# A fourth buffer for the experts' second-layer weights, each load issued four steps ahead instead of three

## The chip, the cores and the metric

The kernel runs on one core of a Trainium2 chip. The metric is the device time of one execution in microseconds (us), lower is better. Before the change it is 457.55 us, the median of three runs (457.02 to 459.05). A core has TensorE (matmuls), VectorE, ScalarE and GpSimd for the rest of the arithmetic, and SyncE, whose queue issues the large transfers between the chip's memory (HBM) and the core's on-chip memory (SBUF). In the profile they are PE, DVE, ACT, POOL and SP; PEld is TensorE's loading of weights.

## What is computed

Three layers, one after the other, all in float32. The first is a retention attention: scores with a decay per head in place of a softmax, over 2 x 8 heads, 576 positions, head size 64. Its output, 1152 tokens of width 512, goes through a layer of 8 experts: a gate picks one expert for each token, and the token passes through that expert's two matrices. The result goes through a normalised, gated feed-forward of width 1536. Cut to the part that the change touches:

```python
logits = x @ w_gate                                  # 1152 x 512 by 512 x 8
expert_idx = np.argmax(logits, axis=1)
...
h = np.maximum(np.einsum('ecd,edf->ecf', disp, w1), 0.0)   # w1: 8 x 512 x 1024
y = np.einsum('ecf,efd->ecd', h, w2)                       # w2: 8 x 1024 x 512
...
out[i] = gate_w[i] * y[expert_idx[i], pos[i]]
```

## The kernel before, in words

The attention comes first (0 to 64 us in the trace). It writes each token's row into a table in HBM that is ordered by expert, so that the rows of one expert lie together. Then the experts run one after the other (about 65 to 219 us), those with the most tokens first, and last the feed-forward.

The experts' weights don't fit in SBUF at once, so they are streamed. An expert's work is cut into four **steps** of 256 hidden columns each, 32 steps in all (`steps`, line 994). A first-layer tile (`w1t`, 1 MB) serves two steps and lives in a ring of three buffers. A second-layer tile (`w2t`, 128 partitions x 2 x 512 float32, 512 KB) serves one step and lives in a ring of three buffers, `w2p` (line 141). The function `load_w2` (line 194) issues the load on SyncE's queue, and `next_w2` (line 983) takes the next tile from the list `w2_q`. The loads of the first three tiles are issued during the attention (`AT_LOADS`, line 34).

A second-layer tile is not used as it comes. So that TensorE can run in a faster format with float32's accuracy, the tile is split in two parts. `w2_hi` (line 753, two instructions at line 759 on ScalarE) makes the rounded part `w2h`, and `w2_lo` (line 762, one instruction at line 768 on VectorE) makes the rest, `w2l`. After both, the tile's buffer is free. Some steps split their first-layer weights as well (lines 782 and 788), and in the others TensorE reads `w1t` as it is (line 848).

The whole program is written out by hand in the order in which each engine is to take it (`manual_schedule`), and the program's loop over the steps (line 1000) sets that order. In step i:

- every second step issues a first-layer load (line 1002);
- `l1` multiplies the first layer of step i on TensorE (lines 841, 843 and 848). It writes the accumulator `hp`, of which there is one, so it waits until the step before has read it;
- `l1_sum`, `h_hi` and `h_lo` add the parts, apply the relu and split the result `h` (lines 857, 858, 871, 877);
- `w2_lo` of step i runs on VectorE, and right behind it `next_w2` issues the next second-layer load;
- `w2_hi` of step i+1 runs on ScalarE;
- `w1_hi` and `w1_lo` of step i+2 run, where that step splits its first layer;
- `l2` of step i-1 multiplies the second layer on TensorE (lines 896 and 897) into accumulators of which there is one set, so an expert's first step waits until `norm_a` has read out the expert before (`y`, line 923);
- between these stand the norms of the expert before, the rows of the expert after next (`load_x`, line 791, read by the transposes at line 809), and, in one step of four, a piece of converting the feed-forward's weights (`bg_ops`).

```python
        if not split(e, j):
            w2_lo(e, j)
        next_w2()
        ...
        for n in nxt:
            for _ in w2_hi(*n):
                pass
```

SyncE takes its queue in order. A second-layer load waits there for the `w2l` that frees its buffer; behind it stand the first-layer loads, the rows and the units of the feed-forward's weights (`st`, line 210). GpSimd issues a few transfers of its own: ten scatters of token numbers (line 988), one in each of steps 4 to 13.

Of the kernel before, what the change touches and what calls it, by code (L numbers as in the profile page):

```python
# [25 lines left out]
TW = 192  # L26
# [63 lines left out]
def kernel(  # L90
# [47 lines left out]
    xnp = ctx.enter_context(tc.tile_pool(name="xnp", bufs=1, side="right"))  # L138
    es_w = ExitStack()
    w1p = es_w.enter_context(tc.tile_pool(name="w1p", bufs=3, side="right"))  # L140
    w2p = es_w.enter_context(tc.tile_pool(name="w2p", bufs=3, side="right"))

    x0p = es_w.enter_context(tc.tile_pool(name="x0p", bufs=1, side="right"))

# [35 lines left out]
    xh = xnp.tile([P, KD, XW], F32R, name="xh")  # L180
    xl = xnp.tile([P, KD, XW], F32R, name="xl")

# [1 line left out]
    w1_t, w2_t, w2_s, w2u = {}, {}, {}, {}  # L184
    st_t = {}

# [7 lines left out]
    def load_w2(e, j):  # L194
        t = w2p.tile([P, 2, DM], F32, tag="w2", name="w2t")
        nc.sync.dma_start(out=t, in_=w2[ds(ex[e], 1), j * 256:(j + 1) * 256, :].rearrange("o (k p) f -> p (o k) f", p=P))
        w2_t[e, j] = t
# [92 lines left out]
            bg_ops(1)  # L290
        conv_tail()

# [1 line left out]
    dec = ap1.tile([P, NP * S], F32, name="dec")  # L294
    ubd = ap1.tile([P, NP, P], F32, name="ubd")
    wid = ap1.tile([P, KD, P + E], F32, name="wid")
# [269 lines left out]
    cnt, kept, inc, off, dn, dinc, zz, key, skey, over, few, perm, skept, offe = (fl[:, i, :] for i in range(14))  # L566
# [70 lines left out]
    def positions(n):  # L637
        for _ in range(min(n, len(pos_q))):
            pos_q.pop(0)()

# [1 line left out]
    def clear_rows(pool, r, r0):  # L642
        at = pool.tile([CW, 1], F32, tag="at", name="vat")
        xr = pool.tile([CW, XC], F32, tag="xr", name="vxr")
        ok = pool.tile([CW, 1], F32, tag="ok", name="vok")
        ri = pool.tile([CW, 1], I32, tag="ri", name="vri")
        tr = cst("trash", CW)[:, 0:1]
        nc.vector.memset(xr, 0.0)
        nc.vector.tensor_scalar(out=ok, in0=tr, scalar1=float(r0 - E * R), scalar2=skept[:CW, r:r + 1], op0=ALU.add, op1=ALU.is_ge)
        nc.vector.tensor_scalar(out=at, in0=perm[:CW, r:r + 1], scalar1=float(R), scalar2=float(r0 - E * R), op0=ALU.mult, op1=ALU.add)  # L650
        nc.vector.scalar_tensor_tensor(out=ri, in0=ok, scalar=at, in1=tr, op0=ALU.mult, op1=ALU.add)
        nc.gpsimd.indirect_dma_start(
            out=tab[:], out_offset=bass.IndirectOffsetOnAxis(ap=ri[:, 0:1], axis=0),
            in_=xr[:], in_offset=None)
# [75 lines left out]
        ints[0:1, 0:E], engines=[ENG.DVE], min_val=0, max_val=NT,  # L730
        skip_runtime_bounds_check_because="prefix sums of expert counts never exceed the number of tokens")

# [1 line left out]
    wA = ctx.enter_context(tc.tile_pool(name="wA", bufs=A_U))  # L734
    stg = ctx.enter_context(tc.tile_pool(name="stg", bufs=ST))
    cvt = ctx.enter_context(tc.tile_pool(name="cvt", bufs=3))
# [54 lines left out]
    def load_x(e):  # L791
        xr = mp1.tile([CW, 2, XC], F32, tag="xr", name="xr")
        w = WIDTHS[e]
        nc.sync.dma_start(out=xr[:w // 2], in_=tab[ds(ex[e] * R, w)].rearrange("(b p) c -> p b c", p=w // 2))
        xr_t[e] = xr
# [187 lines left out]
    def next_w2():  # L983
        if w2_q:
            load_w2(*w2_q.pop(0))
# [9 lines left out]
    for _ in w2_hi(*steps[0]):  # L995
        pass
    load_x(1)
    nps = {}
    positions(8)
    for i, (e, j) in enumerate(steps):  # L1000
# [63 lines left out]
    l2(*steps[-1])  # L1064
    es_w.close()

# [1 line left out]
    GT = 384  # L1068
    phases = [list(range(0, A_U)), list(range(A_U, A_U + PH1)), list(range(A_U + PH1, NF2))]
    order = [(ph, g, f) for ph in range(3) for g in range(NG) for f in phases[ph]]  # L1070
# [154 lines left out]
```

## Time and profile before

| | |
|---|---|
| median of three runs | 457.55 us |
| lowest, highest | 457.02, 459.05 us |
| profiled execution, first to last instruction (its span) | 453.2 us |
| the profiled execution's own time | not recorded beside its span |
| TensorE busy | 432.1 us (95%) |
| VectorE busy | 286.6 us (63%) |
| ScalarE busy | 210.8 us (47%) |
| GpSimd busy | 53.3 us (12%) |
| mean rate of the transfers | 160 GB/s |

Times in the trace count from the first instruction. A matmul's end is modelled, so neighbouring matmuls seem to overlap, and the distance from start to start tells more than the duration. The clock granted to TensorE in the experts' stage is 0.99 of full speed, which is the upper of its two levels, 2.4 GHz. An idle time in the trace stands with what ended it: `[0.96 <-DVE hb L858]` is 0.96 us without work, ended by VectorE's `hb`, line 858.

### The profile page before, as it was taken

The page shows a single profiled execution, that of the slowest core. Times are in us where ns is not written, and L with a number is a line of the kernel's source. Part 1 is how long each engine was busy: PE and PEld are TensorE (multiplying, and loading weights), DVE is VectorE, ACT ScalarE, POOL GpSimd, SP SyncE. Part 2 cuts the span into 40 slices and gives each one's busy share as a digit, 9 for nine tenths or more (in the row PEclk, how much of TensorE's full clock was granted, in tenths as well). Part 3 has the DMA queues.
Part 4 walks back from the last instruction along what each step waited for, and adds up shares of the span by engine and source line. Part 5 has one row for each costly group of instructions (what it writes and reads, how often), then busy time and mean ns, then how long its engine had stood idle before and what let it go on. Part 6 is the DMA issues. An engine that isn't in the chain of part 4 may idle for free.

```text
span 453.2 us, 7828 instructions
## 1 busy us (share of the span) xinstructions
PE 432.1 (95%) x2968; PEld 409.9 (90%) x2968; DVE 286.6 (63%) x677; ACT 210.8 (47%) x453; POOL 53.3 (12%) x45
## 2 busy tenths in 40 slices
PE   5999959999999998999999999999999999999994
PEld 5888859999998988999999999999999999999993
DVE  3899848678787877876588888793873113113212
ACT  3443326677686848766456665361441111111210
POOL 8005210122411011012000000000000002001102
PEclk9999989999999999999999999999999999999998
DMA  8999837897989796666025555251300001000101
GB/s 282 299 282 374 306 112 245 269 294 197 326 171 310 251 303 231 235 229 238 2 90 174 166 165 196 93 171 61 94 0 1 0 2 69 1 1 6 65 0 69
DMA packets 40448, 72.31 MB, mean 160 GB/s; under 512 B 3894, under 2 KB 16566, under 8 KB 40404
## 3 DMA queue, kind: packets, MB, share of 16 engines
q1 hardware_dynamic: 38580, 67.00, 46.5%
q0 software_dynamic: 1824, 4.75, 2.9%
q8 instruction: 25, 0.41, 0.4%
q14 instruction: 19, 0.16, 0.1%
HBM read 65.21 MB, written 6.52 MB: 158 GB/s over the span
## 4 chain that ended last, share of the span: by engine, by line
PE 66%; ACT 8%; DMA 7%; DVE 3%; issue 1%; POOL 1%; POOLq 0%; DVEq 0%; ACTq 0%
PE gv L1098 11%; PE gv L1099 11%; PE gv L1100 11%; PE hp L848 7%; DMA w2t<-in_moe_w_dram 7%; PE o L1132 5%; PE o L1134 5%; PE o L1133 5%; PE acc L896 5%; ACT w2h L759 2%; PE acc L897 2%; PE hp L841 1%; ACT xn L935 1%; ACT w1h L782 1%; ACT xt L817 1%
## 5 line engine op out<-in xcount | busy, mean ns | idle before, releaser
L1098 PE MATMUL gv<-xh,uh 128*128 128x384 f32 x280 | 94.9, 339 | 0.0
L1100 PE MATMUL gv<-xh,ul 128*128 128x384 f32 x280 | 94.7, 338 | 0.0
L1099 PE MATMUL gv<-xl,uh 128*128 128x384 f32 x280 | 94.7, 338 | 0.0
L896 PE MATMUL acc<-h,w2h 128*128 128x384 f32 (+6 forms) x256 | 72.0, 356 | 1.5 <-DVE y L923 1.4
L897 PE MATMUL acc<-h,w2l 128*128 128x192 f32 (+6 forms) x256 | 61.5, 240 | 0.0
L1110 DVE TENSOR_TENSOR sg<-sg,gv 128x384 f32<-128x384 f32 x35 | 19.3, 551 | 63.8 <-PE gv L1100 59.6
L848 PE MATMUL hp<-xt,w1t 128*128 128x192 f32 (+6 forms) x336 | 53.0, 313 | 4.9 <-PEq L713 2.9
L848 PEld LDWEIGHTS hp<-xt,w1t 128*128 128x128 f32 x336 | 49.2, 195 | 5.7 <-DVE ints L604 3.1
L1098 PEld LDWEIGHTS gv<-xh,uh 128*128 128x128 f32 x280 | 52.7, 188 | 1.4
L1099 PEld LDWEIGHTS gv<-xl,uh 128*128 128x128 f32 x280 | 52.7, 188 | 1.4
L1112 ACT ACTIVATE sh<-sg 128x384 fp32r<-128x384 f32 x36 | 18.9, 526 | 73.1 <-DVE sg L1110 73.0
L1100 PEld LDWEIGHTS gv<-xh,ul 128*128 128x128 f32 x280 | 52.7, 188 | 0.0
L896 PEld LDWEIGHTS acc<-h,w2h 128*128 128x128 f32 x256 | 48.1, 188 | 2.1 <-DVE y L923 2.1
L897 PEld LDWEIGHTS acc<-h,w2l 128*128 128x128 f32 x256 | 49.0, 191 | 0.0
L759 ACT ACTIVATE w2h<-w2t 128x512 fp32r<-128x512 f32 x64 | 36.6, 621 | 14.1 <-DMA w2t<-in_moe_w_dram 9.5
L1132 PE MATMUL o<-uh,sh 128*128 128x512 f32 x108 | 42.8, 397 | 0.0
L1134 PE MATMUL o<-uh,sl 128*128 128x512 f32 x108 | 42.7, 396 | 0.0
L1133 PE MATMUL o<-ul,sh 128*128 128x512 f32 x108 | 42.5, 394 | 0.0
L1108 ACT ACTIVATE sg<-gv 128x384 f32<-128x384 f32 x35 | 17.0, 486 | 49.5 <-PE gv L1100 49.5
L768 DVE TENSOR_TENSOR w2l<-w2t,w2h 128x1024 fp32r<-128x1024 f32 x32 | 38.9, 1215 | 0.0
L1147 POOL DMA_INDIRECT out_dram<-part,ids_sb x9 | 8.8, 982 | 215.1 <-DVE part L1145 214.2
L259 ACT ACTIVATE uh<-mag 128x512 fp32r<-128x512 f32 x36 | 22.6, 627 | 14.7 <-DVE mag L251 10.0
(172 smaller groups left out, 723.0 us busy)
## 6 DMA issues: line engine op xcount, KB each, us to landing
w1t<-in_moe_w_dram SPq DMA_DIRECT2D x16, 1024.0 KB, 9.5
w2t<-in_moe_w_dram SPq DMA_DIRECT2D x32, 512.0 KB, 7.1
st<-in_moe_w_gate_dram SPq DMA_DIRECT2D x12, 512.0 KB, 4.6
st<-in_moe_w_val_dram SPq DMA_DIRECT2D x12, 512.0 KB, 4.1
st<-in_moe_w_out_dram SPq DMA_DIRECT2D x12, 512.0 KB, 4.1
qkt<-in_qk_dram SPq DMA_DIRECT2D x6, 512.0 KB, 6.0
kvt<-in_kv_dram SPq DMA_DIRECT2D x6, 512.0 KB, 6.1
tab<-xh SPq DMA_DIRECT2D x9, 193.5 KB, 6.1
```

What stands on the lines that cost most here:

```text
L259: nc.scalar.activation(out=uh[:, s, :], in_=mag, func=ACTF.Copy)
L759: nc.scalar.activation(out=w2_s[e, j][0][:, a, :], in_=t[:, a, :], func=ACTF.Copy)
L768: nc.vector.tensor_tensor(out=lo, in0=t, in1=hi.bitcast(F32), op=ALU.subtract)
L848: nc.tensor.matmul(hp[:, a, 0:w], wt[:, kk, f * FT:(f + 1) * FT], xt[:, kk, :], start=(kk == 0), stop=(kk == KD - 1))
L896: nc.tensor.matmul(ac[d // 2][:, d % 2, 0:2 * w], hi[:, a, d * P:(d + 1) * P], h[:, a].rearrange("p s t -> p (s t)"), start=first, stop=Fa ...
L897: nc.tensor.matmul(ac[d // 2][:, d % 2, 0:w], lo[:, a, d * P:(d + 1) * P], h[:, a, 0, :], start=False, stop=last, skip_group_check=True)
L1098: nc.tensor.matmul(ps[:, 0:GT], w_h, x_h, start=(kk == 0), stop=False)
L1099: nc.tensor.matmul(ps[:, 0:GT], w_h, x_l, start=False, stop=False)
L1100: nc.tensor.matmul(ps[:, 0:GT], w_l, x_h, start=False, stop=(kk == KD - 1))
L1132: nc.tensor.matmul(o, a, uh[:, 2, :], start=(f == fs[0]), stop=False)
L1133: nc.tensor.matmul(o, a, ul[:, 2, :], start=False, stop=False)
L1134: nc.tensor.matmul(o, b, uh[:, 2, :], start=False, stop=(f == fs[-1]))
```

## The change

The ring of second-layer tiles gets a fourth buffer, and one call of `next_w2` is added ahead of the loop, so that each later call takes the tile after the one it took before. In step i the call issues tile i+4 instead of tile i+3. The buffer that it goes into is that of tile i, as before. The other lines of the diff only take out comments.

```diff
-    w2p = es_w.enter_context(tc.tile_pool(name="w2p", bufs=3, side="right"))
+    w2p = es_w.enter_context(tc.tile_pool(name="w2p", bufs=4, side="right"))
...
     for _ in w2_hi(*steps[0]):
         pass
     load_x(1)
+    next_w2()
     nps = {}
     positions(8)
     for i, (e, j) in enumerate(steps):
```

## Rows read from the trace of the kernel before

**Rows 1.** Busy time by stage: length, us of PE, PEld, DVE, ACT, POOL, clock, DMA.

```profile
65.00:219.00 154.00, 150.51 (x1131) 149.23 (x1130) 116.86 (x207) 107.78 (x234) 23.86 (x18) 0.99 0.79 245
...
177.00:205.00 28.00, 28.00 (x234) 28.00 (x232) 22.54 (x41) 20.96 (x47) 3.06 (x2) 1.00 0.71 244
```

**Rows 2.** Waits from 64 to 219 us: engine, line, what it waited for, us in total, times, longest.

```profile
ACT w2h L759 <- DMA w2t<-in_moe_w_dram: 9.5, 4, 3.1
```

**Rows 3.** ScalarE in order of time: start, duration, instruction, and in brackets the idle time before.

```profile
119.30 1.15 ACT L759 ACTIVATE w2h<-w2t 128x512 fp32r<-128x512 f32 x2 [2.26 <-DMA w2t<-in_moe_w_dram]
...
139.71 1.15 ACT L759 ACTIVATE w2h<-w2t 128x512 fp32r<-128x512 f32 x2 [3.10 <-DMA w2t<-in_moe_w_dram]
...
165.65 1.15 ACT L759 ACTIVATE w2h<-w2t 128x512 fp32r<-128x512 f32 x2 [2.59 <-DMA w2t<-in_moe_w_dram]
...
169.96 1.15 ACT L759 ACTIVATE w2h<-w2t 128x512 fp32r<-128x512 f32 x2 [1.57 <-DMA w2t<-in_moe_w_dram]
```

**Rows 4.** TensorE in order of time around its three idle times.

```profile
142.85 0.35 PE L896 MATMUL acc<-h,w2h 128*128 128x340 f32 x1
143.04 0.24 PE L897 MATMUL acc<-h,w2l 128*128 128x170 f32 x1
144.24 0.54 PE L848 MATMUL hp<-xt,w1t 128*128 128x162 f32 x2 [0.96 <-DVE hb L858]
...
167.67 0.24 PE L897 MATMUL acc<-h,w2l 128*128 128x162 f32 x1
168.95 0.40 PE L848 MATMUL hp<-xt,w1t 128*128 128x154 f32 x1 [1.04 <-DVE h L877]
...
170.63 0.69 PE L848 MATMUL hp<-xt,w1t 128*128 128x154 f32 x4
172.71 0.41 PE L896 MATMUL acc<-h,w2h 128*128 128x308 f32 x1 [1.40 <-DVE y L923]
```

**Rows 5.** Waits of SyncE's queue, whole span, same columns as rows 2.

```profile
SPq L196 <- DVE w2l L768: 98.4, 27, 5.2
```

**Rows 6.** SyncE's issues of second-layer loads, then us to landing (first two alike).

```profile
104.39 0.38 SPq L196 DMA_DIRECT2D w2t<-in_moe_w_dram  x1
...
125.08 0.37 SPq L196 DMA_DIRECT2D w2t<-in_moe_w_dram  x1
...
150.44 0.37 SPq L196 DMA_DIRECT2D w2t<-in_moe_w_dram  x1
...
154.52 0.37 SPq L196 DMA_DIRECT2D w2t<-in_moe_w_dram  x1
...
w2t<-in_moe_w_dram SPq DMA_DIRECT2D x1, 512.0 KB, 8.7
...
w2t<-in_moe_w_dram SPq DMA_DIRECT2D x1, 512.0 KB, 3.3
...
w2t<-in_moe_w_dram SPq DMA_DIRECT2D x1, 512.0 KB, 11.1
```

**Rows 7.** The first-layer load in step 0: issue, us to landing, first reader on ScalarE.

```profile
66.30 0.41 SPq L191 DMA_DIRECT2D w1t<-in_moe_w_dram  x1
...
w1t<-in_moe_w_dram SPq DMA_DIRECT2D x1, 1024.0 KB, 6.0
...
84.19 1.13 ACT L782 ACTIVATE w1h<-w1t 128x512 fp32r<-128x512 f32 x2
```

**Rows 8.** Two stretches, then a first-layer load's issue, us to landing, first read.

```profile
105.00:110.00 5.00, 5.00 (x40) 4.99 (x39) 4.79 (x6) 5.00 (x12) 0.01 (x1) 1.00 0.43 31
110.00:126.00 16.00, 16.00 (x116) 15.84 (x115) 12.49 (x23) 10.80 (x24) 6.79 (x4) 1.00 0.98 309
...
105.02 0.37 SPq L191 DMA_DIRECT2D w1t<-in_moe_w_dram  x1
...
w1t<-in_moe_w_dram SPq DMA_DIRECT2D x1, 1024.0 KB, 12.1
...
123.88 0.41 PE L848 MATMUL hp<-xt,w1t 128*128 128x170 f32 x1
```

## The prediction

> **What bounds the kernel now.** I read the busy time by stage first, because the change touches one stage only: the experts, 65 to 219 us. There TensorE is busy 150.51 of 154 us, so 3.49 us is all that it idles, while VectorE and ScalarE have over 37 us of slack each [rows 1]. From 177 to 205 us (the last step of expert 5, expert 6 and the first steps of expert 7) it has no gap at all: 28.00 of 28.00 us. The stage is thus bound by TensorE wherever the loads come in time, and whatever the change brings must come out of TensorE's gaps.
>
> Next I read the waits of the engines in this stage. ScalarE stood 9.5 us, in four waits, for a second-layer weight tile that had not landed [rows 2]. The reader should not take 9.5 us as the gain: ScalarE is not the bound. Its four waits are 2.26, 3.10, 2.59 and 1.57 us long [rows 3], before tiles 11, 15, 20 and 21 (I number the 32 tiles as the 32 steps, four to an expert).
>
> Then TensorE's own order of time around them [rows 4]. After the wait of 3.10 it idles 0.96 us for the sum `hb`, after the 2.59 it idles 1.04 us for `h`, after the 1.57 it idles 1.40 us for `y`. All three are made on VectorE from something that stands behind the late `w2h` split in ScalarE's order of instructions. These three make 3.40 of the 3.49 us. The wait of 2.26 shows no idle time behind it. So ScalarE can be roughly 1.4 to 2 us late before TensorE notices (2.59 less a loss of 1.20, 3.10 less 1.12; the losses are worked out below).
>
> **The change, part by part.**
>
> *The slots.* Each step has one place in SyncE's queue where a second-layer load is issued, behind the wait for that step's `w2l` (27 such waits, 98.4 us in total, the longest 5.2 [rows 5]). In step i it carries tile i+3 now and tile i+4 then. The wait, the instruction that ends it and everything queued behind it (first-layer loads, rows of x, units of the feed-forward) stay as they are; no wait is added on any engine. As sizes and order in the queue are the same, I take the landing time of each slot as it is in this trace and only move the tile in it. Each tile then lands when its predecessor lands now.
>
> *What each late tile finds* [rows 3, 6]. Tile 11 is wanted at 119.30 - 2.26 = 117.04; its new slot is issued at 104.39 and takes 8.7, so it is there at 113.1, 3.9 early. Tile 15 is wanted at 136.61; slot 125.08 + 8.7 = 133.8, 2.8 early. Tile 20 is wanted at 163.06; slot 150.44 + 3.3 = 153.7, 9.3 early. Tile 21 is wanted at 168.39 in this trace, but at 165.80 once the 2.59 ahead of it are gone; slot 154.52 + 11.1 = 165.6, only 0.2 early. With the 1.4 us that TensorE tolerates, that slot may slip by 1.6 us before it costs anything. All four waits go, the last one narrowly.
>
> *What TensorE gets back* [rows 4]. I count from start to start, because the listed idle time begins at a modelled end and leaves out the overlap of neighbours. Neighbours overlap by 0.16 us (142.85 + 0.35 is 143.20, and the next starts at 143.04), so a matmul of L897, 0.24 long, is followed after 0.08 when nothing is late. At 143.04 + 0.08 = 143.12 the next could have started, it did at 144.24: 1.12. At 167.67 + 0.08 = 167.75, started 168.95: 1.20. The group of four at 170.63 lasts 0.69, and with the same overlap the next would start at 171.16; it started at 172.71: 1.55. The sum is 3.87 us. The idle rows alone would give 3.40, and ScalarE's 9.5 us is an upper end that TensorE's 3.49 us of idle time excludes. I take 3.9, nearer to the rows that measure starts.
>
> *What is late next.* In step 19 to 21, tile 21 as above. Otherwise TensorE itself, as from 177 to 205 us.
>
> *The extra load ahead of the loop* (tile 3) now goes out behind the rows of x for expert 1, and the first-layer load issued at 66.30, which takes 6.0 us, moves behind it. A load of this size took 3.3 to 11.1 us [rows 6], so that first-layer load lands at 72.3 + 3.3 at best and 72.3 + 11.1 = 83.4 at worst, and its first reader on ScalarE starts at 84.19 [rows 7]. I cost it at nothing; the cover is these 0.8 to 8.6 us. Tile 3 itself comes earlier than now. A gain is excluded, as nothing waits for it now. SyncE issues one load more here and none in step 28, so the four feed-forward loads behind it go out a step earlier, to no reader that is waiting.
>
> *Memory.* The fourth tile is 2 x 512 x 4 = 4,096 bytes in each partition, beside tiles that keep their readers: cost nothing.
>
> **The sum** is against this execution's span: 453.2 - 3.9 = 449.3 us. The median of the runs stands 4.35 us over this span; I take that as time outside it, which the change does not touch; 449.3 + 4.35 gives 453.6, against 457.55: faster by 0.85%. About 0.5% (2.3 us) is what a measurement can tell from no change.
>
> **A rule against it.** The trace shows loads of this tile landing 8.7 and 11.1 us after issue, and one in 3.3 [rows 6]. The Trainium skill, "DMA: Bandwidth & Descriptors", section "Anatomy of one DMA", fits a DMA's time as 2.0 us plus its bytes over 436 GB/s, on GpSimd's path. As an estimate, that is 3.2 us for 512 KB, so the present lead would be plenty and an earlier issue worth nothing: 457.55. The trace agrees with it for the load of 3.3 us and not for the others, which stood behind other transfers; the rows decide.
>
> **The rivals.**
>
> *The last slot is late* (13%). In step 17's slot a load takes 11.1 us, with 0.2 us to spare. If it takes 2.8 us or more longer, the idle times before 168.95 and 172.71 partly return; at most both, 1.20 + 1.55 = 2.75, leave a gain of 1.12: 456.4. For it: this is the slowest of the slots that I looked up. Against it: TensorE's tolerance.
>
> *Throughput, not lead* (12%). From 110 to 126 the transfers are busy 0.98 of the time, and before that lies a hole of 5 us with 31 GB/s [rows 8]. If the loads are late because the bytes can't come faster, a queue that is one tile ahead eats its lead in the first hole and the waits return: 457.5. Against it: over the stage the share is 0.79 [rows 1], so the lead can be won back, and the needed improvement is only the 1 to 2 us by which ScalarE exceeds TensorE's tolerance. The page's rule, as a mechanism here (a load takes 3.3 us whatever is queued, so lead is no matter), gives the same 457.55; I give it 2% more.
>
> *Slower* (5%). The holes grow. The first-layer load issued at 105.02 goes through the hole, takes 12.1 us and lands at 117.1; TensorE reads it from 123.88 on, 6.8 us later [rows 8]. If one more load waiting in the queue made the hole of 5 us three times as long, this load would be late by 10 - 6.8 = 3.2 us on TensorE itself, and twice that if a later expert meets the same: 453.6 + 6.4 = 460.0. It decides from the point where a hole is longer than 5 + 6.8 = 11.8 us. Against it: the bytes in the queue at any step are the same as now, but for the first step.
>
> *The change does nothing* would need the loads to wait for a later reader than now; the slot's wait is the same instruction, so I give it no share of its own.
>
> **How the numbers follow.** The forecast of 453.6 has 68%. The range must leave out 2 in 10 at most: its lower end is 452.6, from a gain of 5 us if the waits of other executions are longer (the slowest of the three runs is 1.5 us over the median); its upper end, 457.0, takes in the late slot (456.4) and leaves out the rest of throughput and slower. Faster by over 0.5%, under 455.26: 68% and a little of the late slot, 0.70. Within 0.5%: 0.25. Slower: 0.05.
>
> **What would show it.** Right: no wait of ScalarE's L759 for a tile from 100 us on, TensorE's busy time equal to the window in experts 2 to 5, the stage shorter by 3.9 us and the feed-forward shifted as a whole with its length unchanged; the number of waits of SyncE at L196 as now, less one. Wrong: waits at L759 that remain at tiles 20 to 22, TensorE idle for `y` or `h` there, or idle on a first-layer tile; or a stage that is shorter and a feed-forward that is longer.

## The result, and the profile after

The changed kernel takes 450.78 us (median of six runs, 449.99 to 453.54) against 456.48 for the kernel before (six runs, 454.67 to 459.05). The ratio is 0.9892, with a 95% interval of 0.9861 to 0.9922: faster by 1.1%. The forecast was 453.6 us, with a range of 452.6 to 457.0, so the direction was right and the time lies below the range. The profiled execution has a span of 449.3 us, which is the figure that the sum gave (453.2 - 3.9), in part by luck, as the section on the prediction shows. Its own time is 451.24 us, so 1.94 us lies outside the span and not 4.35. The feed-forward is as long as before: from its first matmul to the start of TensorE's last it takes 227.57 us in both kernels.

The busy time by stage of the kernel after, with the columns of [rows 1]; the stage now ends some 4 us earlier, so the first stretch is cut at 215:

```profile
65.00:215.00 150.00, 149.53 (x1130) 149.17 (x1129) 116.63 (x211) 107.99 (x234) 26.45 (x18) 0.99 0.81 252
125.00:145.00 20.00, 20.00 (x154) 20.00 (x153) 17.48 (x29) 16.19 (x36) 6.62 (x4) 1.00 0.99 287
165.00:185.00 20.00, 20.00 (x164) 20.00 (x163) 16.59 (x29) 15.55 (x37) 1.53 (x1) 1.00 0.80 277
```

TensorE idles 0.47 of 150 us, where it idled 3.49 of 154. The two stretches that held its stalls are full.

Its waits from 64 to 219 us, all that TensorE and ScalarE's line 759 have, and SyncE's wait over the whole span (columns of [rows 2, 5]):

```profile
PE hp L848 <- DVE perm_u L592: 0.9, 1, 0.9
PE acc L897 <- DVE w2l L768: 0.5, 1, 0.5
ACT w2h L759 <- ACTq L726: 5.8, 1, 5.8
SPq L196 <- DVE w2l L768: 91.6, 26, 4.7
```

No line says any more that ScalarE waited for a tile to land; the 9.5 us of [rows 2] are gone, and the one wait left at line 759 is the stage's beginning. SyncE stands at line 196 once less than before, as foreseen.

The four slots of [rows 6] in the kernel after, now carrying tiles 11, 15, 20 and 21, first their issues in SyncE's order of time:

```profile
105.42 0.38 SPq L196 DMA_DIRECT2D w2t<-in_moe_w_dram  x1
...
124.93 0.37 SPq L196 DMA_DIRECT2D w2t<-in_moe_w_dram  x1
...
149.04 0.37 SPq L196 DMA_DIRECT2D w2t<-in_moe_w_dram  x1
...
153.12 0.37 SPq L196 DMA_DIRECT2D w2t<-in_moe_w_dram  x1
```

and in the same order their us to landing, from the view of the transfers:

```profile
w2t<-in_moe_w_dram SPq DMA_DIRECT2D x1, 512.0 KB, 9.9
...
w2t<-in_moe_w_dram SPq DMA_DIRECT2D x1, 512.0 KB, 7.3
...
w2t<-in_moe_w_dram SPq DMA_DIRECT2D x1, 512.0 KB, 5.5
...
w2t<-in_moe_w_dram SPq DMA_DIRECT2D x1, 512.0 KB, 11.2
```

The last one is the slot with 0.2 us to spare. It lands at 153.12 + 11.2 = 164.3, and ScalarE in order of time shows how close that is:

```profile
161.61 1.14 ACT L759 ACTIVATE w2h<-w2t 128x512 fp32r<-128x512 f32 x2
162.65 0.70 ACT L826 ACTIVATE xs<-xt 128x616 fp32r<-128x616 f32 x1
163.60 0.77 ACT L972 ACTIVATE xh<-xn 128x680 f32 x1 [0.25 <-DVE xn L968]
164.42 0.43 ACT L871 ACTIVATE h<-hp 128x308 fp32r<-128x308 f32 x1
164.74 1.14 ACT L759 ACTIVATE w2h<-w2t 128x512 fp32r<-128x512 f32 x2
```

The split of tile 21 starts at 164.74 with no idle time before it, 0.4 us after the landing. [rows 3] has 1.57 us of waiting there, behind another 2.59 at tile 20.

### The profile page after: what moved, and what is told of

Same layout as the page of the kernel before. It is cut to its first block, busy times and chain, and to the rows that moved or that the text cites. A ratio compares the mean times of both kernels' runs of the same rounds, so it can differ in the third digit from the quotient of the medians.

```text
span 449.3 us, 7829 instructions
## 1 busy us (share of the span) xinstructions
PE 432.7 (96%) x2968; PEld 411.1 (91%) x2968; DVE 285.3 (63%) x677; ACT 211.1 (47%) x453; POOL 55.9 (12%) x45
## 4 chain that ended last, share of the span: by engine, by line
PE 82%; DVE 1%; POOL 0%; issue 0%; POOLq 0%; DVEq 0%
PE gv L1099 11%; PE gv L1100 11%; PE gv L1101 11%; PE acc L896 11%; PE hp L848 9%; PE o L1133 5%; PE o L1135 5%; PE o L1134 5%; PE acc L897 5%; PE hp L841 4%; PE hp L843 2%; PE tp L809 1%; PE sp L962 1%; POOL out_dram L1148 0%; PE sp L942 0%; PE gw L1100 0%
## 5 line engine op out<-in xcount | busy, mean ns | idle before, releaser
L896 PE MATMUL acc<-h,w2h 128*128 128x384 f32 (+6 forms) x256 | 71.9, 355 | 0.0
L897 PE MATMUL acc<-h,w2l 128*128 128x192 f32 (+6 forms) x256 | 61.6, 240 | 0.5 <-DVE w2l L768 0.5
L848 PE MATMUL hp<-xt,w1t 128*128 128x192 f32 (+6 forms) x336 | 53.5, 315 | 0.9 <-DVE perm_u L592 0.9
L848 PEld LDWEIGHTS hp<-xt,w1t 128*128 128x128 f32 x336 | 50.0, 197 | 1.4 <-DVE perm_u L592 1.4
L897 PEld LDWEIGHTS acc<-h,w2l 128*128 128x128 f32 x256 | 48.9, 191 | 0.8 <-DVE w2l L768 0.8
L896 PEld LDWEIGHTS acc<-h,w2h 128*128 128x128 f32 x256 | 48.1, 188 | 0.0
```

Source lines behind the costliest of these rows:

```text
L848: nc.tensor.matmul(hp[:, a, 0:w], wt[:, kk, f * FT:(f + 1) * FT], xt[:, kk, :], start=(kk == 0), stop=(kk == KD - 1))
L896: nc.tensor.matmul(ac[d // 2][:, d % 2, 0:2 * w], hi[:, a, d * P:(d + 1) * P], h[:, a].rearrange("p s t -> p (s t)"), start=first, stop=Fa ...
L897: nc.tensor.matmul(ac[d // 2][:, d % 2, 0:w], lo[:, a, d * P:(d + 1) * P], h[:, a, 0, :], start=False, stop=last, skip_group_check=True)
```

## The experiments

Two questions were open. Why did the absolute time miss, when the span was right? And what makes the loads late, so that one buffer more is enough? Runs of one group share a chip and the runs of the kernel before that they are compared with. The time of the kernel before differs between groups (456.48, 459.73, 456.87 and 459.48 us), so each result is given as a ratio to the kernel before in its own group, with its 95% interval.

### Both kernels again

No edit: the kernel before.

> The kernel before, unchanged, to see the span of every run beside its time. Theory (the base was wrong): time outside the span is 1.7 to 2.1 us, as in the runs after the change, and the runs differ from each other by their spans (452 to 457 us), because loads are late by different amounts. Rival (a fixed cost): each run's time stands 4.0 to 4.7 us over its span and the spans are within 1 us of 453.2.

Ratio 0.9994 (0.9961 to 1.0026) to itself, median 459.73 us. The profiled execution took 459.21 us with a span of 457.4: 1.81 us outside. Over its 12 runs the time outside is 1.73 to 2.68 us, within the theory's 1.7 to 2.1 in ten of them, and the span 454.5 to 461.7. The rival, 4.0 to 4.7 us, falls. The spans reach past the upper end expected. The profiled one is 4.2 us longer than the first, and the profile shows three reasons. The experts' stage begins at 67.43 instead of 64.29, which the change has no part in: 3.14 us. Its first 32 matmuls run at the lower clock for longer: 0.59. And the stalls cost 0.48 more in all, because the one behind tile 15 is far dearer and the two behind tiles 20 and 21 are milder. ScalarE in order of time, at tile 15:

```profile
144.78 1.15 ACT L759 ACTIVATE w2h<-w2t 128x512 fp32r<-128x512 f32 x2 [4.88 <-DMA w2t<-in_moe_w_dram]
```

The wait is 4.88 us here, where [rows 3] has 3.10. TensorE in order of time behind it:

```profile
146.33 0.24 PE L897 MATMUL acc<-h,w2l 128*128 128x170 f32 x1
149.29 3.51 PE L848 MATMUL hp<-xt,w1t 128*128 128x162 f32 x16 [2.72 <-DVE hb L858]
152.59 1.23 PE L809 MATMUL tp<-cs,xr 77*128 77x77 f32 x8
```

It could have gone on at 146.33 + 0.08 = 146.41 and loses 2.88 us. The busy time of the stretch that follows (columns of [rows 1]):

```profile
150.60:153.90 3.30, 3.30 (x18) 3.26 (x17) 3.04 (x5) 3.30 (x7) 0.00 (x0) 0.50 0.83 281
```

The clock is granted at 0.50 there, the lower level of 1.2 GHz, and the 16 matmuls from 149.29 on take 3.51 us. Behind the shorter stall of the first profile the clock stayed at its upper level. There the same 16 take 2.48 us, as TensorE's order of time shows for the whole group that begins in [rows 4]:

```profile
144.24 2.48 PE L848 MATMUL hp<-xt,w1t 128*128 128x162 f32 x16 [0.96 <-DVE hb L858]
```

So this stall costs 2.88 + 1.03 us, and something more in the transposes behind it, which run at the lower clock too.

> The changed kernel again, on the same chip. Theory: 0.986 to 0.992 of before, spans within 448 to 450 us in nearly every run, no wait of ScalarE for a second-layer tile from 100 us on. Rival (the first result was a chance of the day): ratio above 0.995.

Ratio 0.9885 (0.9842 to 0.9929). The gain repeats. The expectations on the spans and on ScalarE's waits do not hold. On this chip the spans are 450.4 to 455.3 us. The profiled execution is the longest, its experts' stage beginning at 68.53. Two waits are left in the changed kernel. One is of ScalarE for tile 21 (1.93 us, with no idle time of TensorE behind it): this is the last slot coming late, the prediction's first rival, but without a cost. The other is of TensorE for the rows of expert 6:

```profile
170.19 0.74 PE L809 MATMUL tp<-cs,xr 74*128 74x74 f32 x8 [1.32 <-DMA xr<-tab]
```

### Two more profiled executions of the kernel before

No edit.

> The kernel before, one look more. Theory (the first profile was one of its shorter executions): time less span 1.7 to 2.1 us; the experts' stage, from TensorE's first L848 to its last L897, is 155 to 160 us, with idle times of TensorE that sum to 3 to 6 us and, behind one of over 2 us, a stretch of half the granted clock. Rival: stage within 0.5 us of 155.25 again.

> As the run before it, a second look: what differs between two executions of the same program is not the program's doing. Theory: the places and lengths of TensorE's idle times differ between the two, the stage by 0.5 us or more. Rival: same places and lengths within 0.2 us.

Times of 458.61 and 460.77 us, spans of 456.8 and 458.0: 1.81 and 2.77 us outside, the latter more than expected. From TensorE's first L848 to its last L897 the stage is 155.55 and 157.28 us, against 155.25 in the first profile and 156.31 in the run above. The stage of look_a lies within 0.5 us of the first profile's, so its rival holds for the length of the stage. The places of the stalls are the same each time (the waits are for tiles 11, 15, 20 and 21, in look_b for tile 10 too), against what was expected of look_b; their lengths differ, as expected. TensorE's idle time behind tile 15 is 0.96, 2.72, 1.87 and 2.44 us. In the last three it is TensorE's longest after the stage's first matmul, and the clock falls behind it. In look_b, TensorE in order of time and then the busy time of the stretch that follows:

```profile
149.58 3.69 PE L848 MATMUL hp<-xt,w1t 128*128 128x162 f32 x15 [2.44 <-DVE hb L858]
```

```profile
150.40:153.70 3.30, 3.30 (x15) 3.26 (x15) 3.03 (x5) 3.19 (x7) 0.00 (x0) 0.50 0.82 283
```

The first profile was thus the mildest of four executions in its stalls, the only one in which no stall took the clock along. Most of the difference between the spans lies ahead of the stalls, though: the stage starts 2.8 to 3.4 us later in the other three (67.43, 67.65 and 67.09 against 64.29).

### The two halves of the change

```diff
-    w2p = es_w.enter_context(tc.tile_pool(name="w2p", bufs=3, side="right"))
+    w2p = es_w.enter_context(tc.tile_pool(name="w2p", bufs=4, side="right"))
```

> Fourth buffer alone, without the extra call. Theory (the free buffer sets the time of issue, not the place of the call): the load of tile i+3 stands in step i but waits only for the w2l of step i-1, so it goes out at the same moment as in the full change, merely behind the first-layer load of its step; ratio within 0.003 of the full change, 0.986 to 0.993. Rival (the call four steps ahead does it): ratio above 0.996, with the four waits still there.

Ratio 0.9894 (0.9851 to 0.9936), within 0.001 of the full change in the same group. Two waits of ScalarE are left, for tiles 20 and 21, 2.6 us in all, and behind them one idle time of TensorE of 0.66 us.

```diff
     load_x(1)
+    next_w2()
     nps = {}
```

> The extra call alone, with three buffers. Theory: the load of tile i+4 stands in step i but its buffer is free only after the w2l of step i+1, so SyncE stands there and the load goes out no earlier than before; what is queued behind it (first-layer loads, rows) goes out a step later. Ratio 0.998 to 1.01, with waits of 5 to 15 us of ScalarE for tiles. Rival (the place of the call does it): ratio under 0.993.

Ratio 1.0077 (1.0037 to 1.0117). The extra call alone makes the kernel slower. ScalarE's waits are 6.0 us, as expected, but that is not the main loss. The waits from 70 to 230 us:

```profile
ACT w2h L759 <- DMA w2t<-in_moe_w_dram: 6.0, 4, 4.5
PE tp L809 <- DMA xr<-tab: 5.8, 2, 3.8
```

and the first of the two for rows, in TensorE's order of time:

```profile
93.16 0.84 PE L809 MATMUL tp<-cs,xr 90*128 90x90 f32 x8 [2.06 <-DMA xr<-tab]
```

SyncE now stands at line 196 for a buffer that comes free a step later, and the rows of x wait behind it: those of this line are issued 21.7 us after the stage's start (89.25 - 67.55), where the first profile has 15.1 (79.37 - 64.29). TensorE waits for these rows itself. What matters is therefore when the buffer comes free; where the call stands in the program matters only for what queues behind it.

### One buffer more, one less

```diff
-    w2p = es_w.enter_context(tc.tile_pool(name="w2p", bufs=4, side="right"))
+    w2p = es_w.enter_context(tc.tile_pool(name="w2p", bufs=5, side="right"))
...
     load_x(1)
     next_w2()
+    next_w2()
```

> Five buffers and two calls ahead of the loop, so each load goes out five steps ahead. Theory (lead of one more step covers the lateness): nothing is left for a fifth buffer to gain, ratio 0.985 to 0.993 and within 0.003 of the full change; any wait left is for rows of x or none. Rival (loads are short of throughput, so every further buffer helps): ratio under 0.985.

Ratio 0.9882 (0.9846 to 0.9917), the same as with four. TensorE is busy 116.00 of the 116.00 us from 100 to 216, so there is nothing left for a fifth buffer to win.

```diff
-AT_LOADS = {5: [(1, 0, 0)], 6: [(2, 0, 0)], 7: [(2, 0, 1)], 8: [(1, 0, 1), (2, 0, 2)]}
+AT_LOADS = {5: [(1, 0, 0)], 6: [(2, 0, 0)], 7: [(2, 0, 1)], 8: [(1, 0, 1)]}
...
-    w2p = es_w.enter_context(tc.tile_pool(name="w2p", bufs=3, side="right"))
+    w2p = es_w.enter_context(tc.tile_pool(name="w2p", bufs=2, side="right"))
```

> Two buffers, each load issued two steps ahead (the third of the early loads moves into the loop). Theory: each tile lands when its successor lands now, so nearly every tile from step 4 on is late by 1 to 6 us in the first pass; as later issues wait too, the queue empties and a load takes 3.5 to 6 us; ratio 1.02 to 1.10, and where TensorE idles for 2 us or more its granted clock falls to half for some 3.4 us afterwards. Rival (lead hardly matters, as a load takes 3.3 us): ratio under 1.01.

Ratio 1.0489 (1.0427 to 1.055). ScalarE's wait from 70 to 246 us:

```profile
ACT w2h L759 <- DMA w2t<-in_moe_w_dram: 39.0, 19, 6.7
```

The busy time of a stretch inside a stall of TensorE that lasts from 115.5 to 120.3 us (4.82 us idle, for `y`), and of the stretch that follows:

```profile
116.00:119.40 3.40, 0.00 (x0) 0.00 (x0) 0.00 (x0) 2.04 (x6) 0.00 (x0) 1.00 1.02 352
119.50:126.00 6.50, 5.70 (x21) 5.70 (x22) 5.12 (x8) 4.46 (x10) 0.00 (x0) 0.50 0.46 141
```

The loads of the stage in the view of the transfers, with their median us to landing:

```profile
w2t<-in_moe_w_dram SPq DMA_DIRECT2D x30, 512.0 KB, 3.8
```

ScalarE waits 39.0, 9.5 and 0 us for tiles in the profiles with two, three and four buffers (1.9 in the second profile with four). Lead, the time by which a load is issued ahead of its use, is what these loads lack. After the 4.82 us without a matmul the clock is at 0.50 over the next 6.5 us, longer than the 3.4 expected. The load takes 3.8 us at the median where the queue is short, against 7.1 over the kernel with three buffers, so most of the 8 to 11 us of the late loads is time behind other transfers.

### What makes the loads late: the scatters

```diff
-            if 0 <= i - 4 < NTI:
-                scatter_id(i - 4)
+            if 0 <= i - 21 < NTI:
+                scatter_id(i - 21)
```

> Three buffers as before; GpSimd's ten scatters of token numbers go in steps 21 to 30 instead of 4 to 13. Theory (the scatters make the holes in the transfers): no stretch of 3 us with the transfers busy under 0.3 between 100 and 135 us, tiles 7 to 17 land in time, and lateness moves to the steps from 22 on; ratio 0.990 to 1.003. Rival (holes come from elsewhere): holes of 4 to 5 us near 105 and 127 us as before, waits as before, ratio 0.998 to 1.002.

Ratio 1.0003 (0.9971 to 1.0035). The time is the same, but the holes have moved. The busy time of the stretches that held them, in this kernel:

```profile
105.00:110.00 5.00, 5.00 (x40) 4.99 (x39) 4.79 (x6) 5.00 (x12) 0.00 (x0) 1.00 0.82 289
126.00:130.00 4.00, 4.00 (x35) 4.00 (x34) 4.00 (x5) 3.96 (x10) 0.00 (x0) 1.00 0.83 264
```

All five waits of ScalarE for tiles, in its order of time:

```profile
163.95 1.15 ACT L759 ACTIVATE w2h<-w2t 128x512 fp32r<-128x512 f32 x2 [2.56 <-DMA w2t<-in_moe_w_dram]
168.77 1.15 ACT L759 ACTIVATE w2h<-w2t 128x512 fp32r<-128x512 f32 x2 [2.09 <-DMA w2t<-in_moe_w_dram]
196.01 1.15 ACT L759 ACTIVATE w2h<-w2t 128x512 fp32r<-128x512 f32 x2 [2.19 <-DMA w2t<-in_moe_w_dram]
206.34 1.15 ACT L759 ACTIVATE w2h<-w2t 128x512 fp32r<-128x512 f32 x2 [2.97 <-DMA w2t<-in_moe_w_dram]
210.88 1.15 ACT L759 ACTIVATE w2h<-w2t 128x512 fp32r<-128x512 f32 x2 [1.44 <-DMA w2t<-in_moe_w_dram]
```

From 105 to 110 the transfers are busy 0.82 of the time, where [rows 8] has 0.43. Tiles 11 and 15 come in time. The five waits are for tiles 20, 21, 27, 29 and 30: the last three are in the steps to which the scatters went, and so are the new holes (from 202 to 206 us the transfers move 31 and 42 GB/s, right behind four scatters issued from 196.7 on). The scatters make the lateness of tiles 11 and 15. Tiles 20 and 21 are late as ever, so they have another cause.

> The full change with the scatters in steps 21 to 30. Theory (with four buffers TensorE is the bound and holes are covered): within 0.003 of the full change, 0.985 to 0.993. Rival (the holes still cost something): 0.003 or more below the full change.

Ratio 0.9879 (0.9833 to 0.9926), the same as the full change: four buffers cover the scatters wherever they stand.

### What makes the loads late: the rows of expert 6

In the first profile of the kernel before, the transfers nearly stop from 153 to 155 us, though the load of expert 6's rows, issued at 151.07, is still on its way (columns of [rows 1]):

```profile
153.00:155.00 2.00, 2.00 (x17) 2.00 (x16) 2.00 (x4) 1.60 (x4) 0.00 (x0) 1.00 0.10 31
```

A share of 0.10 is 1.6 of the 16 transfer engines. This load is of 2 x 74 rows onto 74 partitions. The Trainium skill, "DMA: Bandwidth & Descriptors", section "Why a DMA increments its semaphore by 16 and not by 1", says that a transfer runs on the largest number of engines up to 16 that divides the outermost dimension of both its source and its destination: by that, two engines for 74, and 16 for the weight tile of 128 partitions issued behind it. The trace agrees: the load is 148 packets of 2,064 bytes, one for each row of 516 numbers. They run from 153.8 to 163.7 us, and for 7.2 of these 9.9 us two of them are on their way at a time. So the weight load issued at 154.52 runs beside them almost to its end, at 165.6.

```diff
-        nc.sync.dma_start(out=xr[:w // 2], in_=tab[ds(ex[e] * R, w)].rearrange("(b p) c -> p b c", p=w // 2))
+        src = tab[ds(ex[e] * R, w)].rearrange("(b p) c -> p b c", p=w // 2)
+        m = w // 32 * 16
+        nc.sync.dma_start(out=xr[:m], in_=src[:m])
+        if m < w // 2:
+            nc.sync.dma_start(out=xr[m:w // 2], in_=src[m:])
```

> Three buffers as before; each load of an expert's rows of x goes out as two transfers, the first over a multiple of 16 partitions, the rest over at most 13. The load of expert 6's rows, 74 partitions, is issued at 151.07 just ahead of the second-layer load that takes 11.1 us. Theory (that transfer runs on few of the 16 queues of the transfer engines and the weight load behind it waits for those): the load of step 17 takes 3.3 to 7 us, ScalarE waits for no tile of expert 5, TensorE has no idle time near 169 and 173 us; ratio 0.990 to 0.998. Rival (weight loads are slow there for another reason): the load of step 17 still takes over 9 us, ratio 0.998 to 1.002.

The edit splits the loads of every expert's rows. Ratio 0.997 (0.9942 to 0.9999): a gain of 0.3%, with an interval that barely leaves out no change. The 148 packets of expert 6's rows now take 1.8 us, from 158.9 to 160.7. The load of step 17 goes out at 160.18; its landing is not recorded. ScalarE's splits of tiles 11, 15, 20 and 21 in this kernel:

```profile
124.17 1.15 ACT L759 ACTIVATE w2h<-w2t 128x512 fp32r<-128x512 f32 x2 [1.89 <-DMA w2t<-in_moe_w_dram]
...
145.39 1.15 ACT L759 ACTIVATE w2h<-w2t 128x512 fp32r<-128x512 f32 x2 [3.90 <-DMA w2t<-in_moe_w_dram]
...
168.62 1.13 ACT L759 ACTIVATE w2h<-w2t 128x512 fp32r<-128x512 f32 x2
...
171.60 1.14 ACT L759 ACTIVATE w2h<-w2t 128x512 fp32r<-128x512 f32 x2
```

Tile 20 is split without a wait 8.4 us after its issue, so its load took no longer than that, where it took 11.1; whether it took the 3.3 to 7 us expected stays open. Tile 21 is split without a wait too, and TensorE has no idle time in expert 5. Tiles 11 and 15 wait as before, so the other experts' rows are not what makes them late. The lateness thus has two causes, each shown by taking it away alone: the scatters for 11 and 15, the rows of expert 6 for 20 and 21.

> The full change with the rows loaded in two transfers. Theory (with four buffers TensorE is the bound and the slow rows are covered, but for a rare late row): 0 to 0.003 below the full change, 0.984 to 0.991. Rival (the slow rows still cost the changed kernel something): over 0.003 below the full change.

Ratio 0.9903 (0.9867 to 0.9938), no better than the full change alone. No version beats the four buffers: 0.9892, 0.9885, 0.9894, 0.9882, 0.9879 and 0.9903 can't be told apart.

## Why the prediction was wrong in the time and right in the mechanism

- **The slots: right.** "I take the landing time of each slot as it is in this trace": forecast 8.7, 8.7, 3.3 and 11.1 us, measured 9.9, 7.3, 5.5 and 11.2. All four waits went, and tile 21 had 0.4 us where 0.2 was worked out.
- **What TensorE gets back: the term too small, the span right by luck.** The forecast of 3.87 us equals the difference of the spans, but the stalls were worth 4.9. TensorE at the start of the stage and at the start of the feed-forward, first before, then after:

```profile
64.29 7.12 PE L848 MATMUL hp<-xt,w1t 128*128 128x192 f32 x32 [2.88 <-PEq L713]
...
71.52 0.36 PE L896 MATMUL acc<-h,w2h 128*128 128x384 f32 x1
...
219.37 0.38 PE L1098 MATMUL gw<-xh,uh 128*128 128x384 f32 x1
```

```profile
63.86 7.89 PE L848 MATMUL hp<-xt,w1t 128*128 128x192 f32 x32 [0.95 <-DVE perm_u L592]
...
72.39 0.36 PE L897 MATMUL acc<-h,w2l 128*128 128x192 f32 x1 [0.47 <-DVE w2l L768]
72.58 0.36 PE L896 MATMUL acc<-h,w2h 128*128 128x384 f32 x1
...
215.51 0.38 PE L1099 MATMUL gw<-xh,uh 128*128 128x384 f32 x1
```

From the second matmul of L896 on, which stands behind everything that differs at the start, it is 147.85 us before (71.52 to 219.37) and 142.93 after (72.58 to 215.51): 4.92 less. The profiles of ring5, late_ids_after and rows_split_after give 142.92 for the same distance, so this is the stage without stalls. The kernel after gave 1.49 us of it away at the start, where 32 matmuls took 7.89 us against 7.12 at a lower clock and TensorE waited once for `w2l`, and it began 0.43 us earlier; 4.92 - 1.49 + 0.43 makes the 3.86 of the spans. The start is not the change's doing: late_ids_before, which lacks it, takes 8.22 us for the 32 matmuls and idles 0.57 us at the same place. Start to start and matmul by matmul, the three stalls of [rows 4] give back 4.13 us. The rest, 0.8, lies in four places where the prediction saw none, because no idle time is listed between matmuls there: behind 123.70, 131.13, 149.25 and 151.32 the next one or two came late, by 0.07 to 0.29 us in all at each.
- **The price of a stall in other executions: missed.** The sum priced one execution. Three more show longer stalls behind tile 15 and half the clock after them; over the distance above they take 148.34, 148.16 and 149.23 us, so their stalls were worth 5.4, 5.2 and 6.3. By the ratio the measured gain is 0.0108 x 456.48 = 4.9 us, over 3.9, and the medians differ by 5.7. The profile had no stall that took the clock along, so the term was not in it; three runs over its time could have been read as a warning.
- **The base: the step that failed.** "The median of the runs stands 4.35 us over this span; I take that as time outside it." In the 59 runs of the kernel before that stood beside the experiments it is 1.73 to 3.09 us, and their spans run from 451.9 to 461.4. By these the profiled execution took about 455.1 us and at most 456.3, and was no median run: the three runs then known were slower executions. With 1.9 us the same sum gives 449.3 + 1.9 = 451.2, which is the profiled execution's 451.24. That is 2.4 of the 2.8 us by which the forecast missed the median. The range hung on the same base: its lower end of 452.6 was 457.55 less 5. What made those three runs slower was not seen. Later profiles show that the stalls vary, and the start of the experts' stage still more: it is at 63.1 to 65.1 us on one chip, at 67.4 to 68.9 and at 67.1 to 69.5 on two others. Why it goes with the chip is not shown.
- **The extra load ahead of the loop at nothing: right.** With two such loads in ring5, TensorE has no idle time within the stage over 0.3 us, and the 0.47 us in step 0 of the kernel after has its like in late_ids_before, without such a load.
- **The rivals.** The late slot did not come in the first profile of the changed kernel, though 0.4 us was all that kept it off for ScalarE. It came in rep_after, 1.93 us late, and cost TensorE nothing, as the tolerance of 1.4 to 2 us that the prediction worked out would have it. Throughput falls with ring5 and ring2: the bytes are the same, a fifth buffer changes nothing, and with two the waits grow. That lead is no matter, the rival drawn from the Trainium skill ("DMA: Bandwidth & Descriptors", "Anatomy of one DMA"), falls with ring2 as well; the 3.2 us estimated by that section's fit is near what a load takes when little is ahead of it, 3.3 us in [rows 6] and 3.8 at the median of ring2. The slower case did not come; its kind, a wait of TensorE for another transfer of the same queue, did in call_only.

## What to carry to other kernels

Price a wait at the engine that bounds the stage and from start to start, and say from which executions: a stall that is 1 us in one execution can be 2.7 us and half a clock in the next. Read starts and not only listed idle times: here 3.40 us were listed where the stalls cost 4.9. Take the time outside the span from runs that have both a time and a span, not from a median of other runs. When a stream of loads is late at the same few tiles each time, look for what stands ahead of these in the queue; a deeper ring covers it, if the free buffer and not only the call comes earlier.

## What the runs showed of the hardware that was not expected

Behind stalls of 1.87, 2.44 and 2.72 us (the kernel before, three executions) TensorE's granted clock was 0.50 over the next 3.3 us, behind one of 4.82 us (two buffers) over the next 6.5 us, and 16 matmuls took 3.51 instead of 2.48 us. Behind one of 1.91 us, with the scatters moved, the clock did not fall. A transfer onto 74 partitions went out two packets at a time for most of its 9.9 us, and the 512 KB load behind it took 11.1 us; split over 64 and 10 partitions the same packets took 1.8 us, and the load behind took at most 8.4. Scatters of 4-byte numbers were followed by 5 us in which the transfers moved 31 GB/s, and such holes moved with them when they were put elsewhere.
